# Signs written from the scaled words, and one softmax normalization per attention step for both query blocks

## The chip, the cores and the metric

The kernel runs on one core of a Trainium2 chip. The metric is the device time of one execution in microseconds; a change counts by the median of several executions. All times below are of that core. Engine names: PE is TensorE (PEld its weight loads), DVE is VectorE, ACT is ScalarE, POOL is GpSimd, SP is SyncE, which here only issues DMAs.

## What is computed

Causal attention over a window of keys plus a few sink keys, then two feed-forward layers on its output.

```python
scores = scale * q @ k.T                       # q, k, v: (2, 8, 768, 64)
keep = is_sink | ((rel >= 0) & (rel < window)) # n_sink 4, window 128
scores = where(keep, scores, -1e9)
a = exp(scores - max(scores))
x = (a / (sum(a) + 1e-9)) @ v                  # -> (1536, 512)
h = maximum(x @ w_in, 0);  x = h * h @ w_out   # 512 -> 2048 -> 512
h = x @ w_in2
out = (P(h) / (Q(h) + 1e-6)) @ w_out2          # P of degree 3, Q of degree 2 in |h|
```

The weights of the feed-forward layers arrive as float64, so every weight word is 8 bytes in HBM.

## The kernel before

**Attention** runs in 24 steps (2 batches, 3 pairs of 128-row query blocks, 4 pairs of heads). A step (`attention`, L304 to L391) is a generator with four pieces. The first two pieces are one query block each (`qb`): PE writes the scores of two heads to PSUM (L329 to L332), DVE adds the mask and takes the row maximum (L340, L341), ACT takes the exponential in place in `e` and sums the row (L348), DVE adds the guard and takes the reciprocal of two sums (L349, L350), and POOL multiplies the block's 320 columns by it (L352). The third piece transposes `e` on PE (`pt`, `sx`, L357 and L360) and lets POOL split it (L366, L367); the fourth multiplies with the values (`xo`, L382 to L386) and writes `xh` and `xl`, which the feed-forward part reads.

**Weights.** A chunk is one of 16 slices of `w_in` and `w_out` of a layer, 32 chunks in all (`load_chunk`, L292); it is loaded in two halves of 128x512 float64 words, 512 KB each. `narrowed` (L53) turns a half into float32: a DMA brings the raw words to `wr` (3 buffers), ACT multiplies the upper 32-bit words by 2^-112 into `t` (tile `wt`, 2 buffers, L63), ACT writes their signs, as the upper half of a zeroed word, into one of two sign tiles (L65), DVE shifts the lower words and adds the sign (L66, in place in `wr`), and DVE shifts `t` and adds that (L67). ACT then rounds to `wh` (L299) and POOL takes the rest, `wl` (L300). After that the half's `wt` buffer is free; its `wr` buffer is free after L67.

**Feed-forward.** 114 units, numbered here from 0: units 0 to 35 (256 tokens wide, 6 chunks, run among the attention steps), 36 to 65 (the rest of the first layer, 512 wide) and 66 to 113 (the second layer). A unit has 12 matmuls to `h` (L400), an activation on ACT, DVE and POOL (`squared_relu`: `sq`, L128 on ACT and L130 on DVE; then `gh` and `gl`, L407 and L409), and 12 matmuls to `acc` (L439 or L441). A unit's `h` is made two or three units ahead of its `acc`. There are 11 chunk slots, so chunks are loaded in bursts: 14 halves at the start, and then as the last use of a chunk frees its slot: around units 33 to 46, 50 to 55, 66 to 76 and 82 to 91.

**Order.** Each engine runs its instructions strictly in order. The order is set when the program is built: a list scheduler with a timeline model of the engines places the instructions of all generators, so a change in one instruction's inputs moves others on all engines. POOL, ACT and DVE serve attention, weights and units from one queue each.

Of the kernel before, what the change touches and what calls it, by code (L numbers as in the profile page):

```python
# [10 lines left out]
F16 = mybir.dt.float16  # L11
# [3 lines left out]
ALU = mybir.AluOpType  # L15
# [5 lines left out]
P = 128  # L21
# [7 lines left out]
GUARD = 1e-9  # L29
# [11 lines left out]
def f32(ap):  # L41
    return ap.bitcast(F32)
# [10 lines left out]
def narrowed(nc, pool, src, n, signs):  # L53

    raw = pool.tile([P, 512, 2], U32, tag="wr", name=f"wr{n}", bufs=3)
    nc.sync.dma_start(raw.rearrange("p c w -> p (c w)"), src.bitcast(U32))
    lo, hi = raw[:, :, 0], raw[:, :, 1]
    t = pool.tile([P, 512], U32, tag="wt", name=f"wt{n}")
    s = signs[0]
    signs.append(signs.pop(0))  # L60


    nc.scalar.mul(f32(t), f32(hi), 2.0**-112)  # L63

    nc.scalar.mul(s.bitcast(F16).rearrange("p (c w) -> p c w", w=2)[:, :, 1], f32(hi), 2.0**-112)  # L65
    nc.vector.scalar_tensor_tensor(out=lo, in0=lo, scalar=29, in1=s, op0=ALU.logical_shift_right, op1=ALU.bitwise_or)  # L66
    nc.vector.scalar_tensor_tensor(out=t, in0=t, scalar=3, in1=lo, op0=ALU.logical_shift_left, op1=ALU.bitwise_or)  # L67
    return f32(t)
# [107 lines left out]
def banded(ctx, tc, const, qk0, qk1, vb, vs, ns_f, win_f, wp, ab, scalars, out):  # L176
    nc = tc.nc
# [114 lines left out]
    def load_chunk(L, pool=wpool):  # L292
        home[L] = pool
        h = pool.tile([P, 1024], F32R, tag="wh", name=f"wh{L}")
        lo = pool.tile([P, 1024], F32R, tag="wl", name=f"wl{L}")
        for i in range(2):
            c = slice(i * 512, (i + 1) * 512)
            t = narrowed(nc, wraw, wp[L][:, c], f"{L}_{i}", signs)
            nc.scalar.copy(h[:, c], t)  # L299
            nc.gpsimd.tensor_tensor(out=lo[:, c], in0=t, in1=f32(h[:, c]), op=ALU.subtract)  # L300
        wh[L], wl[L] = h, lo


    def attention(bb, j, hp):  # L304

        n = f"{bb}_{j}_{hp}"
        nm = at.tile([P, 4], F32, tag="nm", name=f"nm{n}")
        sm = at.tile([P, 4], F32, tag="sm", name=f"sm{n}")
        rs = at.tile([P, 4], F32, tag="rs", name=f"rs{n}")
        W = P + SK  # L310

        e = at.tile([P, 2, 2 * W], F32, tag="e", name=f"e{n}")
        qk, kl, v = loaded[bb, j, hp]

        for qb in range(2):
            first = j == 0 and qb == 0
            nk = W if first else K0
            ss = []
            for hd in range(2):
                if hd == 0:  # L320
                    off = W * qb if j else 0
                else:
                    off = P if first else (W * (1 - qb) if j else 0)
                s = ps_at.tile([P, 512], F32, tag="at", name=f"s{n}_{qb}{hd}")
                cols = slice(qb * P, (qb + 1) * P)
                if kl is None:

                    rows = slice(hd * D, (hd + 1) * D)
                    nc.tensor.matmul(s[:, :nk], lhsT=qk[rows, cols], rhs=qk[rows, 256 + off : 256 + off + nk], start=True, stop=True)  # L329
                else:  # L330
                    nc.tensor.matmul(s[:, :nk], lhsT=qk[hd][:, cols], rhs=qk[hd][:, 256 + off : 256 + off + nk], start=True, stop=False)
                    nc.tensor.matmul(s[:, :nk], lhsT=qk[hd][:, cols], rhs=kl[hd][:, off : off + nk], start=False, stop=True)  # L332
                ss.append(s)
            for hd, s in enumerate(ss):
                u = 2 * qb + hd

                lo = 0 if hd == 0 or first else P
                if not first:
                    prev, own = (s[:, 0:P], s[:, W:K0]) if hd == 0 else (s[:, W:K0], s[:, 0:P])
                    nc.vector.copy_predicated(prev, own_u, own)  # L340
                nc.vector.tensor_tensor_reduce(  # L341
                    out=e[:, qb, hd * W : (hd + 1) * W], in0=s[:, lo : lo + W], in1=add[min(2 * j + qb, 2)][:, SK * (1 - hd) : SK * (1 - hd) + W],
                    scale=-SCALE, scalar=3.0e38, op0=ALU.add, op1=ALU.min, accum_out=nm[:, u : u + 1])
            c = slice(2 * qb, 2 * qb + 2)
            for hd in range(2):
                u = 2 * qb + hd
                eu = e[:, qb, hd * W : (hd + 1) * W]
                nc.scalar.activation(eu, eu, AF.Exp, bias=nm[:, u : u + 1], scale=-1.0, accum_out=sm[:, u : u + 1])  # L348
            nc.vector.tensor_scalar(out=rs[:, c], in0=sm[:, c], scalar1=GUARD, scalar2=None, op0=ALU.add)  # L349
            nc.vector.reciprocal(rs[:, c], rs[:, c])  # L350
            eq = e[:, qb, :].rearrange("p (h w) -> p h w", h=2)
            nc.gpsimd.tensor_tensor(out=eq, in0=eq, in1=rs[:, c].unsqueeze(2).to_broadcast([P, 2, W]), op=ALU.mult)  # L352
            yield
        pt = ps_at.tile([P, 4, P], F32, tag="at", name=f"pt{n}")
        for u in range(4):
            c0 = 0 if u < 2 else W + SK
            nc.tensor.matmul(pt[:, u, :], lhsT=e[:, u % 2, c0 : c0 + P], rhs=ident, is_transpose=True, start=True, stop=True)  # L357
        sx = ps_at.tile([P, 256], F32, tag="at", name=f"sx{n}")
        for qb in range(2):
            nc.tensor.matmul(sx[:, qb * P : (qb + 1) * P], lhsT=e[:, qb, P : 2 * P], rhs=ident, is_transpose=True, start=True, stop=True)  # L360

        pT = at.tile([P, 4, 2, P], F32, tag="pT", name=f"pT{n}", bufs=1)
        pa = at.tile([P, 4, P], F32, tag="pa", name=f"pa{n}", bufs=1)
        sT = at.tile([P, 256], F32R, tag="sT", name=f"sT{n}")
        nc.scalar.copy(pa, pt)
        nc.gpsimd.affine_select(out=pT[:, :, 1, :], in_=pa, pattern=[[0, 4], [1, P]], compare_op=ALU.is_ge, fill=0.0, base=0, channel_multiplier=-1)  # L366
        nc.gpsimd.affine_select(out=pT[:, :, 0, :], in_=pa, pattern=[[0, 4], [-1, P]], compare_op=ALU.is_gt, fill=0.0, base=0, channel_multiplier=1)  # L367

        half = slice(0, 2 * SK)
        nc.scalar.copy(sT[half], sx[half])  # L370
        nc.vector.tensor_tensor(out=sT[2 * SK :], in0=sx[half], in1=f32(sT[half]), op=ALU.subtract)
        yield
        xo = ps_at.tile([P, 256], F32, tag="at", name=f"xo{n}")
        pf = pT.rearrange("p (h q) o c -> p h (q o c)", q=2)
        nb = 2 if j == 0 else 3

        jobs = [(nb - 2, 0, 256, P), (nb - 1, P, 256, 3 * P)]
        if j:
            jobs.append((0, 0, P, 0))
        for i, c0, c1, o in jobs:  # L380
            for hd in range(2):
                nc.tensor.matmul(xo[64 * hd : 64 * hd + 64, c0:c1], lhsT=v[:, i, hd * D : (hd + 1) * D],  # L382
                                 rhs=pf[:, hd, o : o + c1 - c0], start=c1 - c0 == 256, stop=False, skip_group_check=True)
        vh, vl = vst[bb]
        nc.tensor.matmul(xo, lhsT=vh[:, hp, :], rhs=sT, start=False, stop=False, skip_group_check=True)  # L385
        nc.tensor.matmul(xo, lhsT=vl[:, hp, :], rhs=sT, start=False, stop=True, skip_group_check=True)  # L386
        t0 = bb * S + j * 256
        g, c0 = t0 // 512, t0 % 512
        nc.scalar.copy(xh[g][:, hp, c0 : c0 + 256], xo)
        nc.vector.tensor_tensor(out=xl[g][:, hp, c0 : c0 + 256], in0=xo, in1=f32(xh[g][:, hp, c0 : c0 + 256]), op=ALU.subtract)  # L390
        yield  # L391
# [99 lines left out]
    def att_pieces():  # L491
        live = {}
        for t in range(len(todo) + 2):
            for s_ in (t, t - 1, t - 2):
                if s_ < 0 or s_ >= len(todo):
                    continue
                if s_ == t:
                    live[s_] = attention(*todo[s_])
                    if fetch:
                        load_pair(*fetch.pop(0))  # L500
                    for _ in range(2):
                        next(live[s_])
                        yield
                else:
                    next(live[s_])
                    yield
            if t >= 2:
                done[t - 2] = True
# [226 lines left out]
```

## Time and profile before

| | us |
|---|---|
| median of 3 runs (lowest, highest) | 687.01 (686.88, 688.39) |
| the profiled execution | 685.88 |
| its span, first to last instruction | 684.2 |
| PE busy | 648.0 (95%) |
| DVE busy | 467.9 (68%) |
| ACT busy | 460.1 (67%) |
| POOL busy | 401.5 (59%) |

The profiled execution is 1.7 us longer than its span, and 1.1 us below the median of the runs. A busy PE does not mean a PE at its peak, since matmuls overlap in the pipeline; how many matmuls a stretch holds says more. In the rows, "x" is a count, ns after a comma a mean, and an arrow in brackets names what ended an idle time. SPq is the queue of DMA issues on SP.

### The profile page before, as it was taken

What the parts mean: (1) busy time and instruction counts of PE and PEld (TensorE: products, weight loads), DVE (VectorE), ACT (ScalarE), POOL (GpSimd) and SP (SyncE); (2) the same over time, 40 slices, a digit from 0 to 9 for tenths busy, and PEclk for the clock granted to TensorE, in tenths of its full rate; (3) what the DMA queues carried; (4) which work ended last, traced back from release to release, by engine and by line L of the source; (5) the groups of instructions that cost most, each with busy time, mean ns of one, the idle gap of its engine ahead of it and who ended that gap; (6) DMA issues with size and microseconds to landing.
All of it is one profiled execution on the core that took longest, in us unless ns stands there. A gap on an engine that the chain in (4) does not pass through costs nothing.

```text
span 684.2 us, 10131 instructions
## 1 busy us (share of the span) xinstructions
PE 648.0 (95%) x3376; PEld 528.2 (77%) x3376; DVE 467.9 (68%) x969; ACT 460.1 (67%) x938; POOL 401.5 (59%) x367
## 2 busy tenths in 40 slices
PE   4799999999999997999999998899998999999995
PEld 2456779999999875888778886688887888888884
DVE  7878855879842897427631279976699777577674
ACT  6767755777654876427542489886899866766761
POOL 4757855788753776327454579654577644544441
PEclk9999999999999999899999999999999999999998
DMA  7546632354200645204500033200030000001011
GB/s 249 186 134 184 204 90 69 103 135 131 67 25 1 210 160 182 65 1 137 171 0 1 0 124 103 82 1 1 1 123 32 0 1 1 0 1 61 3 61 68
DMA packets 25725, 54.16 MB, mean 79 GB/s; under 512 B 2880, under 2 KB 11072, under 8 KB 25664
## 3 DMA queue, kind: packets, MB, share of 16 engines
q1 hardware_dynamic: 25664, 53.43, 24.5%
q8 instruction: 29, 0.48, 0.3%
q14 instruction: 32, 0.26, 0.1%
HBM read 50.27 MB, written 3.15 MB: 78 GB/s over the span
## 4 chain that ended last, share of the span: by engine, by line
PE 63%; DVE 16%; ACT 8%; DMA 7%; issue 3%; POOL 2%; DVEq 0%; POOLq 0%; ACTq 0%
PE h L400 27%; PE acc L441 14%; PE acc L439 13%; DMA wr<-in_wp 6%; DVE wt L67 5%; DVE wr L66 4%; PE xo L382 3%; ACT sign L65 2%; PE pt L357 1%; PE s L329 1%; ACT wh L299 1%; ACT wt L63 1%; PE xo L385 1%; PE s L332 1%; POOL wl L300 1%
## 5 line engine op out<-in xcount | busy, mean ns | idle before, releaser
L409 POOL TENSOR_TENSOR gl<-sq,gh 128x256 fp32r<-128x256 f32 (+1 forms) x66 | 72.0, 1093 | 80.3 <-ACT gh L407 45.8
L164 POOL TENSOR_TENSOR z<-z,u 128x512 f32<-128x512 f32 x48 | 63.6, 1326 | 84.8 <-ACT z L163 81.5
L300 POOL TENSOR_TENSOR wl<-wt,wh 128x512 fp32r<-128x512 f32 x64 | 91.4, 1439 | 19.9 <-ACT wh L299 19.9
L66 DVE SCALAR_TENSOR_TENSOR wr<-wr,sign 128x512 uint32<-128x512 uint32 x64 | 64.2, 1003 | 19.6 <-ACT sign L65 19.5
L409 POOL TENSOR_TENSOR gl<-z,gh 128x512 fp32r<-128x512 f32 x47 | 62.1, 1322 | 24.8 <-ACT gh L407 21.2
L67 DVE SCALAR_TENSOR_TENSOR wt<-wt,wr 128x512 uint32<-128x512 uint32 x64 | 68.4, 1069 | 10.9 <-ACT wt L63 10.3
L130 DVE TENSOR_TENSOR sq<-sq,h 128x256 f32<-128x256 f32 (+1 forms) x66 | 35.5, 538 | 58.9 <-ACT sq L128 58.1
L439 PE MATMUL acc<-gh,wh 128*128 128x256 f32 (+1 forms) x264 | 66.2, 339 | 5.6 <-ACT sq L128 4.1
L65 ACT ACTIVATE sign<-wr 128x512 f16<-128x512 f32 x64 | 50.6, 790 | 24.6 <-DMA wr<-in_wp 24.4
L439 PE MATMUL acc<-gl,wh 128*128 128x256 f32 (+1 forms) x264 | 64.9, 336 | 0.5 <-POOL gl L409 0.5
L439 PE MATMUL acc<-gh,wl 128*128 128x256 f32 (+1 forms) x264 | 64.7, 334 | 0.0
L170 DVE SCALAR_TENSOR_TENSOR z<-z,con,h 128x512 f32<-128x512 f32 x48 | 35.8, 745 | 41.6 <-ACT h L169 40.1
L400 PE MATMUL h<-xh,wh 128*128 128x256 f32 (+1 forms) x264 | 61.6, 347 | 0.5 <-DVE sq L130 0.5
L128 ACT ACTIVATE sq<-h 128x256 f32<-128x256 f32 (+1 forms) x66 | 31.5, 477 | 45.3 <-PE h L400 34.5
L441 PE MATMUL acc<-wh,gh 128*128 128x512 f32 x192 | 60.2, 393 | 1.2 <-ACT gh L407 1.2
L441 PE MATMUL acc<-wl,gh 128*128 128x512 f32 x192 | 59.6, 390 | 0.0
L400 PE MATMUL h<-x2h,wh 128*128 128x512 f32 x192 | 53.9, 398 | 4.6 <-DVE z L172 4.6
L400 PE MATMUL h<-xl,wh 128*128 128x256 f32 (+1 forms) x264 | 58.2, 337 | 0.0
L400 PE MATMUL h<-xh,wl 128*128 128x256 f32 (+1 forms) x264 | 58.2, 338 | 0.0
L441 PE MATMUL acc<-wh,gl 128*128 128x512 f32 x192 | 57.6, 389 | 0.0
L439 PEld LDWEIGHTS acc<-gh,wh 128*128 128x128 f32 x264 | 44.5, 192 | 13.4 <-ACT wh L299 4.8
L352 POOL TENSOR_TENSOR e<-e,rs 128x320 f32<-128x320 f32 x48 | 37.2, 778 | 28.0 <-DVE rs L350 20.4
(104 smaller groups left out, 1591.9 us busy)
## 6 DMA issues: line engine op xcount, KB each, us to landing
wr<-in_wp SPq DMA_DIRECT2D x64, 512.0 KB, 3.7
qkr<-in_qk SPq DMA_DIRECT2D x32, 176.0 KB, 3.1
v<-in_vb SPq DMA_DIRECT2D x16, 192.0 KB, 2.7
out<-accsb SPq DMA_DIRECT2D x12, 256.0 KB, 2.1
qkr<-in_qk SPq DMA_DIRECT2D x8, 352.0 KB, 3.5
qkr<-in_qk SPq DMA_DIRECT2D x16, 136.0 KB, 2.8
qkr<-in_qk SPq DMA_DIRECT2D x4, 272.0 KB, 5.0
v<-in_vb SPq DMA_DIRECT2D x8, 128.0 KB, 3.6
```

The lines of the kernel that those rows point to most:

```text
L65: nc.scalar.mul(s.bitcast(F16).rearrange("p (c w) -> p c w", w=2)[:, :, 1], f32(hi), 2.0**-112)
L66: nc.vector.scalar_tensor_tensor(out=lo, in0=lo, scalar=29, in1=s, op0=ALU.logical_shift_right, op1=ALU.bitwise_or)
L67: nc.vector.scalar_tensor_tensor(out=t, in0=t, scalar=3, in1=lo, op0=ALU.logical_shift_left, op1=ALU.bitwise_or)
L130: nc.vector.tensor_tensor(out=r, in0=r, in1=h, op=ALU.mult)
L164: nc.gpsimd.tensor_tensor(out=z, in0=z, in1=u, op=ALU.mult)
L170: nc.vector.scalar_tensor_tensor(out=z, in0=z, scalar=con[:, 2:3], in1=h, op0=ALU.add, op1=ALU.mult)
L300: nc.gpsimd.tensor_tensor(out=lo[:, c], in0=t, in1=f32(h[:, c]), op=ALU.subtract)
L352: nc.gpsimd.tensor_tensor(out=eq, in0=eq, in1=rs[:, c].unsqueeze(2).to_broadcast([P, 2, W]), op=ALU.mult)
L400: nc.tensor.matmul(h[:, :n], lhsT=w_[:, k * P : (k + 1) * P], rhs=x_[:, k, c0 : c0 + n], start=p_ + k == 0, stop=p_ + k == 5)
L409: eng.tensor_tensor(out=gl[:, :n], in0=y, in1=f32(gh[:, :n]), op=ALU.subtract)
L439: nc.tensor.matmul(acc[m][:, :n], lhsT=w_[:, 512 + m * P : 512 + (m + 1) * P], rhs=g_[:, :n], start=st, stop=sp, skip_group_check=True)
L441: nc.tensor.matmul(acc[m], lhsT=g_[:, m * P : (m + 1) * P], rhs=w_[:, 512:1024], start=st, stop=sp)
```

## The change

Two edits. In `narrowed`, the sign activation reads `t`, the already scaled upper words, instead of the raw upper words. `t` is contiguous, the raw words stand 8 bytes apart; the value that is written is the same. In `attention`, the guard, the reciprocal and the multiplication by it are issued once per step, after the exponentials of both query blocks, over 4 sums and 640 columns instead of twice over 2 sums and 320 columns.

```diff
-    nc.scalar.mul(s.bitcast(F16).rearrange("p (c w) -> p c w", w=2)[:, :, 1], f32(hi), 2.0**-112)
+    nc.scalar.mul(s.bitcast(F16).rearrange("p (c w) -> p c w", w=2)[:, :, 1], f32(t), 1.0)
...
-            c = slice(2 * qb, 2 * qb + 2)
...
-            nc.vector.tensor_scalar(out=rs[:, c], in0=sm[:, c], scalar1=GUARD, scalar2=None, op0=ALU.add)
-            nc.vector.reciprocal(rs[:, c], rs[:, c])
-            eq = e[:, qb, :].rearrange("p (h w) -> p h w", h=2)
-            nc.gpsimd.tensor_tensor(out=eq, in0=eq, in1=rs[:, c].unsqueeze(2).to_broadcast([P, 2, W]), op=ALU.mult)
+            if qb:
+                nc.vector.tensor_scalar(out=rs, in0=sm, scalar1=GUARD, scalar2=None, op0=ALU.add)
+                nc.vector.reciprocal(rs, rs)
+                eq = e.rearrange("p q (h w) -> p (q h) w", h=2)
+                nc.gpsimd.tensor_tensor(out=eq, in0=eq, in1=rs.unsqueeze(2).to_broadcast([P, 4, W]), op=ALU.mult)
```

The exponential moves from L348 to L347; the other lines named here keep their numbers. The scheduler orders every engine anew. Two places follow.

DVE in the first attention step (names end in batch_pair_headpair and a buffer number; `s` are scores, `nm` maxima, `sm` and `rs` sums and reciprocals). Before:

```order
L340 COPY_PREDICATED s_0_0_11_180<-own_u,s_0_0_11_180 128x128
L349 TENSOR_SCALAR rs_0_0_165<-sm_0_0_164 128x2
L341 ISA e_0_0_166,nm_0_0_163<-s_0_0_11_180,add_116 128x160
L341 ISA nm_0_0_163 128x1
L341 ISA e_0_1_258,nm_0_1_255<-s_0_1_00_259,add_115 128x160
L341 ISA nm_0_1_255 128x1
L350 RECIPROCAL rs_0_0_165<-rs_0_0_165 128x2
```

Now:

```order
L340 COPY_PREDICATED s_0_0_11_177<-own_u,s_0_0_11_177 128x128
L341 ISA e_0_0_166,nm_0_0_163<-s_0_0_11_177,add_116 128x160
L341 ISA nm_0_0_163 128x1
L341 ISA e_0_1_255,nm_0_1_252<-s_0_1_00_256,add_115 128x160
L341 ISA nm_0_1_252 128x1
L341 ISA e_0_1_255,nm_0_1_252<-s_0_1_01_258,add_115 128x160
L341 ISA nm_0_1_252 128x1
L349 TENSOR_SCALAR rs_0_0_165<-sm_0_0_164 128x4
L350 RECIPROCAL rs_0_0_165<-rs_0_0_165 128x4
```

The first query block's guard and reciprocal are gone, and the step's only pair stands behind the maxima of the next step. Counted over the whole order of DVE, ahead of the L130 of unit 2 there were 16 L66, 15 L67 and 18 L350, and there are now 14, 13 and 8; ahead of that of unit 8 there were 19 L66, 16 L67 and 23 L350, and now 16, 16 and 11. Three signs (L65) that ACT wrote ahead of unit 8, before a buffer of `wt` was free for them, stand behind unit 32 now.

ACT in the second burst of weights, from the activation L128 of unit 41 to that of unit 42 (`wr15_1` is the second half of chunk 15). Before:

```order
L128 ACTIVATE sq_3499<-h_3484 128x512
L299 CAST wh14_3290<-wt14_0_3294 128x512
L299 CAST wh14_3290<-wt14_1_3303 128x512
L407 CAST gh_3465<-sq_3467 128x512
L65 ACTIVATE sign1_94<-wr15_1_3321 128x512
L63 ACTIVATE wt15_0_3314<-wr15_0_3312 128x512
L65 ACTIVATE sign0_93<-wr16_0_3332 128x512
L63 ACTIVATE wt15_1_3323<-wr15_1_3321 128x512
L299 CAST wh15_3310<-wt15_0_3314 128x512
L128 ACTIVATE sq_3531<-h_3516 128x512
```

Now:

```order
L128 ACTIVATE sq_3427<-h_3412 128x512
L299 CAST wh13_3198<-wt13_0_3202 128x512
L407 CAST gh_3393<-sq_3395 128x512
L63 ACTIVATE wt13_1_3211<-wr13_1_3209 128x512
L65 ACTIVATE sign1_94<-wt13_1_3211 128x512
L63 ACTIVATE wt14_0_3222<-wr14_0_3220 128x512
L65 ACTIVATE sign0_93<-wt14_0_3222 128x512
L128 ACTIVATE sq_3459<-h_3444 128x512
```

Before, ACT had written the sign of a half, and sometimes of the next, before its `t`; now the sign stands behind its `t`, and at the same unit the weights are one to two chunks further back. Counted over the whole order of ACT, 26 L63 stood ahead of unit 40, 36 ahead of unit 44 and 36 ahead of unit 46; now 25, 32 and 36. In the burst at units 50 to 55 it is 36 ahead of unit 50 and 46 ahead of unit 55, before and now. Ahead of units 66 and 74 it was 49 and 56 and is 48 and 56; the last 8 stand ahead of unit 88 before and ahead of unit 90 now.

## Rows read from the trace of the kernel before

**Rows 1.** The page: the span.
```profile
span 684.2 us, 10131 instructions
```

**Rows 2.** Stages: us, then busy us (count) of PE, PEld, DVE, ACT, POOL; PEclk, DMA, GB/s.
```profile
0.00:85.00 85.00, 68.14 (x318) 44.83 (x319) 70.30 (x233) 61.59 (x171) 56.17 (x64) 0.98 0.60 193
85.00:205.00 120.00, 120.00 (x995) 108.81 (x994) 85.75 (x307) 79.27 (x240) 84.77 (x110) 1.00 0.33 88
...
260.00:280.00 20.00, 15.40 (x57) 11.71 (x56) 14.02 (x19) 12.53 (x23) 10.82 (x9) 0.83 0.52 172
280.00:305.00 25.00, 25.00 (x110) 20.35 (x109) 7.22 (x11) 7.19 (x12) 6.43 (x5) 1.00 0.05 19
305.00:345.00 40.00, 38.46 (x168) 30.98 (x167) 26.05 (x31) 26.61 (x45) 23.94 (x17) 1.00 0.39 132
...
395.00:440.00 45.00, 40.98 (x176) 32.43 (x175) 41.35 (x53) 40.93 (x70) 35.81 (x25) 1.00 0.34 117
...
490.00:530.00 40.00, 38.23 (x166) 30.77 (x165) 35.89 (x46) 37.58 (x65) 29.68 (x22) 1.00 0.20 66
```

**Rows 3.** The chain that ended last, followed back from 85 us: shares, two pieces.
```profile
by line: DMA wr<-in_wp 10.9%; DVE wr L66 8.5%; DVE wt L67 6.1%; PE s L329 5.9%; ACT e L348 5.7%; ACT sign L65 5.7%; PE xo L382 5.3%; DVE rs L349 4.7%; issue 4.1%; PE h L400 3.9%; DMA raw<-in_nw 3.6%; DVE e L341 2.9%; DVE s L340 2.7%; PE pt 
...
54.99 4.41 DMA wr<-in_wp
...
69.40 4.88 DMA wr<-in_wp
```

**Rows 4.** Stages of L349 alone: us, DVE busy us (count), then as in rows 2.
```profile
0.00:40.00 40.00, 4.33 (x9) 1.00 0.60 200
40.00:80.00 40.00, 4.55 (x9) 0.99 0.60 188
```

**Rows 5.** The same of L350.
```profile
0.00:40.00 40.00, 1.42 (x9) 1.00 0.60 200
40.00:80.00 40.00, 1.47 (x9) 0.99 0.60 188
```

**Rows 6.** Timeline of DVE and of POOL: start us, us, engine, line, operation.
```profile
17.09 1.23 DVE L349 TENSOR_SCALAR rs<-sm 128x2 f32<-128x2 f32 x1
...
14.91 3.39 POOL L300 TENSOR_TENSOR wl<-wt,wh 128x512 fp32r<-128x512 f32 x2
```

**Rows 7.** Line L352: ns min/median/max, who waited (us, times); two in the timeline.
```profile
L352 POOL TENSOR_TENSOR e<-e,rs x48: 712/722/1192, 10.3 to 196.1; 128x320 f32<-128x320 f32 x48
...
  PEld pt L357: 2.3, 3
...
152.33 1.40 POOL L352 TENSOR_TENSOR e<-e,rs 128x320 f32<-128x320 f32 x2 [0.83 <-DVE rs L349]
```

**Rows 8.** Groups by line of the narrowing: busy us, mean ns; idle before.
```profile
L66 DVE SCALAR_TENSOR_TENSOR wr<-wr,sign 128x512 uint32<-128x512 uint32 x64 | 64.2, 1003 | 19.6 <-ACT sign L65 19.5
...
L65 ACT ACTIVATE sign<-wr 128x512 f16<-128x512 f32 x64 | 50.6, 790 | 24.6 <-DMA wr<-in_wp 24.4
...
L63 ACT ACTIVATE wt<-wr 128x512 f32<-128x512 f32 x64 | 42.3, 663 | 4.4 <-POOL wl L300 4.2
...
L299 ACT CAST wh<-wt 128x512 fp32r<-128x512 f32 x64 | 38.9, 617 | 11.5 <-DVE wt L67 11.4
```

**Rows 9.** The chain between bursts: one unit's matmuls (start us, us).
```profile
285.62 2.75 PE acc L439 x12
288.37 2.80 PE h L400 x12
```

**Rows 10.** Timeline of SP's queue, from 195 us: the second burst's DMA issues.
```profile
221.88 56.64 SPq L56 DMA_DIRECT2D wr<-in_wp  x20
```

**Rows 11.** Timeline of ACT and PE where PE stood longest in that burst.
```profile
270.29 0.78 ACT L65 ACTIVATE sign<-wr 128x512 f16<-128x512 f32 x1 [1.43 <-DMA wr<-in_wp]
...
271.95 0.59 ACT L128 ACTIVATE sq<-h 128x512 f32<-128x512 f32 x1
272.53 0.76 PE L439 MATMUL acc<-gh,wh 128*128 128x512 f32 x1 [4.05 <-ACT sq L128]
```

## The prediction

> **What bounds the kernel now.** I read the page first, then busy time by stage, then the chain inside the stages that are not full, then single lines. The span is 684.2 us [rows 1]; the stages [rows 2] show three kinds of stretch. To 85 us PE does 318 matmuls in 68 busy us while DVE is busy for 70.3 of 85 us: this is the start, in which attention and the first seven chunks share DVE and ACT. From 85 to 205 us PE is busy without a gap, and all other engines have at least 28% to spare. Behind that PE is full but for four stretches, which are the bursts of weights. A full stretch holds 110 matmuls in 25 us, 0.227 us each. By that price PE loses 20 - 57 x 0.227 = 7.1 us from 260 to 280, 1.9 from 305 to 345, 5.0 from 395 to 440 and 2.3 from 490 to 530 us: 16.3 us in all. In the first of these the granted clock is 0.83 over the stretch: the stall of 4.05 us [rows 11] is followed by matmuls at the lower of the two levels, 1.2 instead of 2.4 GHz, and part of the 7.1 us is that.
>
> So the end moves only if the start gets shorter, or the four bursts lose less or more. Between them nothing can be gained on DVE, ACT or POOL.
>
> **The start: one normalization instead of two.** L349 and L350 run 18 times each to 80 us and take 4.33 + 4.55 and 1.42 + 1.47 us [rows 4, 5], 11.8 us in all. Half of them go: 5.9 us of DVE, the upper bound of the gain. The lower bound is nothing, if something other than DVE ends the stage. The chain up to 85 us [rows 3] gives L349 4.7%, which is 4.0 us; half of that is 2.0, and with a part of the reciprocals I take **-3**.
>
> The multiplication on POOL takes 0.72 us for 320 columns, and two of them back to back 1.40 us [rows 7]. Over 640 columns I take 1.40 us. POOL saves next to nothing (24 x 0.04, about 1 us of an engine with room). But the transposes now wait for a multiplication that begins only behind both blocks and is 1.40 - 0.72 = 0.68 us longer. PE waited for L352 only 3 times, 2.3 us in all [rows 7]; all three can get longer by 0.68, which bounds this at 0 to +2.0; I take **+0.7**. From 85 to 205 us I cost it at nothing: PE has units to run there, and the transposes stand no earlier in PE's order than before. If that cover failed, 14 steps would cost 0.68 each, 9.5 us.
>
> **The start: the sign behind t.** A half's sign used to start when its DMA landed; now t comes first, 0.66 us [rows 8]. Reading contiguous words may make the sign cheaper, by 0.663 - 0.617 = 0.05 us if reading is what separates t from the cast L299, and by 0.17 at most, if it became as short as L299. I take 0.05, 3 us of ACT over 64 halves, which nothing waits for. The chain of the start goes through two DMAs of raw words that a sign then waits for [rows 3]; each gets 0.66 us longer: **+1.2** (0 to +3.5, if all five rounds of 16 halves through 3 buffers showed it). In the other direction, three signs and their L66 leave the start (19 ahead of unit 8, now 16): 3 x 0.79 us of ACT and 3 x 1.0 us of DVE [rows 8], between 0 and -3.0; **-1**. They return in the burst, where they count below. Sum of the start: -3 + 0.7 + 1.2 - 1 = **-2.1**, between -8.9 and +5.5.
>
> **The bursts.** A raw buffer goes round: DMA, ACT, L66, L67, and the next DMA is issued from SP's queue when L67 frees it. In the second burst 20 issues take 56.64 us [rows 10], 2.83 us per half. With three buffers, 0.66 us more per round is 0.22 us more per half: 3.05. A unit takes 2.75 + 2.80 = 5.55 us of PE [rows 9]. Before, ACT's order has 10 halves between the activations of units 40 and 44; they take 28.3 us where four units take 22.2, so PE falls 6.1 us behind, which is most of its 7.1. The rows show how: L128 of unit 43 stands behind a sign that waits for its DMA and behind two casts, and PE waits 4.05 us for it [rows 11]. Now 11 halves stand between units 40 and 46: 33.6 us against 33.3, so PE would hardly fall behind, and the drop of the clock would go with the stall. The bounds are -7.1 (all of it) and +4.4 (20 halves by 0.22, nothing else changed). I take **-4.5**, not the full 6, since port and DMA waits scatter by more than the 0.3 us of margin.
>
> In the burst at units 50 to 55 the order keeps two halves per unit, so its 10 halves get 10 x 0.22 = 2.2 us slower; the lead of `h` over `acc` has room for a part: **+1.5** (0 to +2.2). In the two bursts of the second layer DVE and ACT are each busy for over 40 of 45 us [rows 2] and the change takes nothing from DVE there; the last one is spread over two more units: **-0.5** together (-3 to +3).
>
> **The sum** is -2.1 - 4.5 + 1.5 - 0.5 = -5.6 us against the profiled execution's own 685.9 us, so 680.3. That execution lies 1.1 us under the median of the runs shown, 687.0; carried over, the median becomes **681.4 us**.
>
> **A rule that speaks against it.** DVE's L349 has only 2 columns, and yet it took 1.23 us at 17.09, and ended within 0.02 us of POOL's L300 pair [rows 6]: a small DVE instruction stands until POOL is through. One multiplication of 1.40 us can hold it twice as long in one piece as one of 0.72. The Trainium skill, page "SBUF — State Buffer", section "SBUF: two separate sides", says that DVE and GpSimd share a port pair as an exclusive lock for a whole instruction, the loser blocking fully; by this rule the trace agrees, since L349 waits and does not merely slow down. It is a rival below.
>
> **Rivals.** (1) *Everything comes through*: the start gains its 5.9 + 3.0 and the burst its 7.1, so 670 to 675 us. For it: DVE is the busiest engine of the start. Against: two DMA links and PE's own pieces stand in that chain. 14%. (2) *No difference*: the start is held by the weights, and what DVE gives up is taken by the longer way of each half, while the new order meets the same waits: 685.7 to 688.3 us. For it: the DMA and the four narrowing steps are the largest part of the chain of the start. 13%. (3) *Slower, by the wait of the sign for t in the bursts*: the 48 halves that come behind the start, by 0.22 us, are +10.6; less the 2.1 of the start, and with no other gain in the second burst, the time is 695; with half of the 10.6, 690. It decides where halves come slower than one per 2.8 us (half a unit) while the order asks for two per unit, that is in units 50 to 55 first. For it: all four bursts already lose time. Against: the order now asks for halves later. 17%. (4) *The longer hold of DVE by POOL*: ten steps of the start by 0.7 us, +7.0, and the sum becomes +1.4: 688.4 us. For it: the row of L349 above. Against: the number of DVE instructions that can be held falls as well. 6%. That the change does not do what it says can be left out, since the order shows 24 pairs for 48.
>
> **How the numbers follow.** The forecast, between 676 and 685.6 us, has 50%. About 0.2% (1.4 us) is what a measurement of this kernel can tell from no change. Faster is the forecast and (1), 0.64; the same is (2), 0.13; slower are (3) and (4), 0.23. For the range I leave out most of (1) and the worse half of (3): 675 to 690 us.
>
> **What would show it.** In the profile after: 24 L349 and L350 on DVE, with some 6 us less to 80 us; L352 at 1.3 to 1.5 us; the sign at 0.7 to 0.8 us, behind its t; PE gapless from about 83 us; no stall of over 2 us near unit 43 and a granted clock of 1.00 there; a rate of 3.0 to 3.1 us per issue in the second burst. Wrong would be: PE gapless no earlier than now, a stall of several us in units 50 to 55, or halves that come at well over 3.1 us.

## The result and the profile after

The changed kernel takes **665.6 us** (665.3 to 666.5, 4 runs) where the kernel before, timed beside it, took 686.9 us (684.9 to 688.4): a ratio of **0.969**, 95% interval 0.967 to 0.972. It is faster by 21 us. The forecast was 681.4 us, between 675 and 690: the sign was right, the size was not. The profiled execution took 665.9 us.

The page of the changed kernel: its span, busy time by engine, and the chain that ended last, by engine.

```profile
span 663.8 us, 10100 instructions
...
PE 638.2 (96%) x3376; PEld 522.7 (79%) x3376; DVE 455.6 (69%) x921; ACT 460.2 (69%) x938; POOL 394.6 (59%) x343
...
PE 76%; ACT 9%; DVE 8%; issue 3%; POOL 2%; DMA 1%; SPq 0%; DVEq 0%; POOLq 0%; ACTq 0%
```

The stages of the changed kernel, as in [rows 2].

```profile
0.00:85.00 85.00, 68.37 (x356) 45.10 (x356) 64.48 (x213) 61.58 (x171) 54.27 (x55) 0.92 0.58 187
85.00:205.00 120.00, 120.00 (x1017) 110.97 (x1017) 82.20 (x278) 77.85 (x240) 82.46 (x96) 1.00 0.33 92
...
260.00:280.00 20.00, 19.73 (x85) 15.58 (x84) 14.94 (x20) 14.54 (x25) 12.58 (x9) 1.00 0.41 142
305.00:345.00 40.00, 40.00 (x174) 32.49 (x173) 22.41 (x32) 22.55 (x38) 22.36 (x16) 1.00 0.32 106
395.00:440.00 45.00, 43.96 (x188) 34.80 (x187) 44.62 (x61) 43.01 (x73) 36.33 (x26) 1.00 0.23 82
490.00:530.00 40.00, 40.00 (x174) 32.51 (x174) 36.69 (x53) 36.46 (x62) 25.93 (x20) 1.00 0.08 27
```

By the price of the forecast (0.227 us per matmul) the four stretches of the bursts now lose 0.7, 0.5, 2.3 and 0.5 us, 4.0 in all, where they lost 16.3; the windows are the same, though the bursts now begin 7 to 17 us earlier. The start has 356 matmuls to 85 us instead of 318, but at a clock of 0.92 instead of 0.98.

Where the 21 us came from is read from the units' activations (L128, L159) in ACT's timeline, of one profiled execution of each kernel. Those of units 0, 24, 48, 66 and 113, the last, before:

```profile
58.05 0.36 ACT L128 ACTIVATE sq<-h 128x256 f32<-128x256 f32 x1
...
186.75 0.39 ACT L128 ACTIVATE sq<-h 128x256 f32<-128x256 f32 x1 [0.24 <-PE h L400]
...
296.81 0.60 ACT L128 ACTIVATE sq<-h 128x512 f32<-128x512 f32 x1 [3.14 <-PE h L400]
...
399.29 0.58 ACT L159 ACTIVATE u<-h 128x512 f32<-128x512 f32 x1
...
665.94 0.58 ACT L159 ACTIVATE u<-h 128x512 f32<-128x512 f32 x1
```

The same five now:

```profile
54.75 0.39 ACT L128 ACTIVATE sq<-h 128x256 f32<-128x256 f32 x1
...
180.12 0.38 ACT L128 ACTIVATE sq<-h 128x256 f32<-128x256 f32 x1
...
282.87 0.60 ACT L128 ACTIVATE sq<-h 128x512 f32<-128x512 f32 x1 [2.71 <-PE h L400]
...
383.23 0.59 ACT L159 ACTIVATE u<-h 128x512 f32<-128x512 f32 x1
...
645.26 0.58 ACT L159 ACTIVATE u<-h 128x512 f32<-128x512 f32 x1
```

At unit 24 the start is over and PE is full. The start gave 6.6 us, the stretch behind it with its four bursts 14.0 us: 7.3 to unit 48 (the second burst of weights), 2.1 to unit 66 (the burst at units 50 to 55) and 4.6 to unit 113 (the two bursts of the second layer). Each run below has the same split. The kernel before took between 682.9 and 691.7 us in its runs, so what is read from one execution of it is uncertain by some us. The parts behind the start repeat better: among the runs with the changed sign in the bursts they agree within 1.5 us, but for o1_behind between units 24 and 48.

The steps of the normalization in the changed kernel: first L349 to 40 and to 80 us, as in [rows 4].

```profile
0.00:40.00 40.00, 1.09 (x4) 0.93 0.63 207
40.00:80.00 40.00, 1.36 (x5) 0.90 0.56 175
```

The same of L350, as in [rows 5].

```profile
0.00:40.00 40.00, 0.69 (x4) 0.93 0.63 207
40.00:80.00 40.00, 0.87 (x5) 0.90 0.56 175
```

L352, as in [rows 7], and the last row of who waited for it.

```profile
L352 POOL TENSOR_TENSOR e<-e,rs x24: 1246/1253/1689, 11.5 to 188.5; 128x640 f32<-128x640 f32 x24
...
  PE pt L357: 4.6, 3
```

Before, PE itself never waited for L352; the row of [rows 7] is of weight loads (PEld), 2.3 us, which are 6.5 us now. DVE saved 11.8 - 4.0 = 7.8 us to 80 us, more than the 5.9 that I had as the upper bound, and yet the start gained less than that. The narrowing's lines in the changed kernel, as in [rows 8]:

```profile
L66 DVE SCALAR_TENSOR_TENSOR wr<-wr,sign 128x512 uint32<-128x512 uint32 x64 | 66.5, 1039 | 35.7 <-ACT sign L65 35.4
...
L65 ACT ACTIVATE sign<-wt 128x512 f16<-128x512 f32 x64 | 50.5, 789 | 0.8
L63 ACT ACTIVATE wt<-wr 128x512 f32<-128x512 f32 x64 | 42.7, 667 | 10.6 <-POOL wl L300 8.1 <-DMA wr<-in_wp 2.3
L299 ACT CAST wh<-wt 128x512 fp32r<-128x512 f32 x64 | 39.2, 618 | 22.8 <-DVE wt L67 21.8 <-PE acc L439 0.8
```

The sign itself is no cheaper (789 ns for 790). What is gone is ACT's 24.4 us of waiting for a DMA at the sign; `t`, now in front, waits 2.3 us for a DMA and otherwise, 8.1 us, for a `wt` buffer. A part of the idle time has only moved: at the cast L299 ACT now waits 21.8 us for DVE, where it was 11.4 [rows 8].

### The profile page after: what moved, and what is told of

Read it like the earlier page. It is cut to its first block, busy times and chain, and to the rows that moved or that the text cites. A ratio compares the mean times of both kernels' runs of the same rounds, so it can differ in the third digit from the quotient of the medians.

```text
span 663.8 us, 10100 instructions
## 1 busy us (share of the span) xinstructions
PE 638.2 (96%) x3376; PEld 522.7 (79%) x3376; DVE 455.6 (69%) x921; ACT 460.2 (69%) x938; POOL 394.6 (59%) x343
## 4 chain that ended last, share of the span: by engine, by line
PE 76%; ACT 9%; DVE 8%; issue 3%; POOL 2%; DMA 1%; SPq 0%; DVEq 0%; POOLq 0%; ACTq 0%
PE h L400 34%; PE acc L439 17%; PE acc L441 15%; PE xo L382 3%; DVE wr L66 3%; DVE wt L67 2%; ACT sign L65 1%; ACT wt L63 1%; PE pt L357 1%; PE s L329 1%; PE s L332 1%; PE xo L385 1%; PE s L331 1%; ACT z L163 1%; ACT wh L299 1%
## 5 line engine op out<-in xcount | busy, mean ns | idle before, releaser
L300 POOL TENSOR_TENSOR wl<-wt,wh 128x512 fp32r<-128x512 f32 x64 | 89.0, 1397 | 40.9 <-ACT wh L299 38.9
L66 DVE SCALAR_TENSOR_TENSOR wr<-wr,sign 128x512 uint32<-128x512 uint32 x64 | 66.5, 1039 | 35.7 <-ACT sign L65 35.4
L130 DVE TENSOR_TENSOR sq<-sq,h 128x256 f32<-128x256 f32 (+1 forms) x66 | 35.4, 538 | 49.1 <-ACT sq L128 48.5
L67 DVE SCALAR_TENSOR_TENSOR wt<-wt,wr 128x512 uint32<-128x512 uint32 x64 | 64.4, 1006 | 3.4
L128 ACT ACTIVATE sq<-h 128x256 f32<-128x256 f32 (+1 forms) x66 | 31.3, 474 | 42.5 <-PE h L400 32.1
L400 PE MATMUL h<-xh,wl 128*128 128x256 f32 (+1 forms) x264 | 56.8, 334 | 0.0
L299 ACT CAST wh<-wt 128x512 fp32r<-128x512 f32 x64 | 39.2, 618 | 22.8 <-DVE wt L67 21.8
L400 PE MATMUL h<-x2l,wh 128*128 128x512 f32 x192 | 53.5, 396 | 0.0
L400 PE MATMUL h<-x2h,wl 128*128 128x512 f32 x192 | 53.2, 396 | 0.0
```

What stands on the lines that cost most here:

```text
L128: nc.scalar.activation(r, h, AF.Relu)
L130: nc.vector.tensor_tensor(out=r, in0=r, in1=h, op=ALU.mult)
L400: nc.tensor.matmul(h[:, :n], lhsT=w_[:, k * P : (k + 1) * P], rhs=x_[:, k, c0 : c0 + n], start=p_ + k == 0, stop=p_ + k == 5)
```

## Experiments

Three theories stood at first. **A**: a sign that stands ahead of its `t` in ACT's order waits for its DMA there, and activations that PE needs stand behind it. **B**: the sign behind `t` makes each half longer (the forecast's view), and the gain is the softmax's. **C**: the gain is the contiguous source, or a lucky order. All runs, each timed beside the kernel before, with the split as above ("start" to the activation of unit 24, "rest" from there to unit 113, then the three parts of the rest; us against the trace of the kernel before):

| run | median us | ratio, 95% interval | start | rest | 24 to 48 | 48 to 66 | 66 to 113 |
|---|---|---|---|---|---|---|---|
| changed kernel | 665.63 | 0.969 (0.967 to 0.972) | -6.6 | -14.0 | -7.3 | -2.1 | -4.6 |
| e1_sign | **658.71** | 0.960 (0.954 to 0.965) | -15.4 | -11.9 | -6.2 | -2.1 | -3.6 |
| e2_softmax | 687.65 | 1.000 (0.997 to 1.003) | +3.3 | -1.9 | -2.5 | -0.3 | +0.8 |
| e3_order | 667.08 | 0.972 (0.967 to 0.978) | -10.0 | -9.5 | -7.1 | -2.6 | +0.2 |
| e3_hold | 673.70 | 0.981 (0.976 to 0.986) | -3.4 | -8.8 | -0.7 | -3.1 | -4.9 |
| g1_early | 667.88 | 0.972 (0.968 to 0.977) | -6.3 | -12.9 | -6.2 | -2.1 | -4.6 |
| g2_late | 658.88 | 0.959 (0.955 to 0.963) | -14.1 | -14.1 | -7.3 | -2.1 | -4.6 |
| f1_pool | 669.03 | 0.973 (0.969 to 0.977) | -3.4 | -13.3 | -7.6 | -2.1 | -3.6 |
| f2_dve | 666.70 | 0.969 (0.965 to 0.973) | -6.6 | -13.3 | -7.6 | -2.1 | -3.6 |
| k1_first | 674.87 | 0.983 (0.978 to 0.988) | -14.7 | +2.1 | -0.7 | 0.0 | +2.7 |
| k2_rest | 673.66 | 0.980 (0.976 to 0.983) | +0.2 | -12.9 | -6.3 | -2.1 | -4.6 |
| m_warm | 668.48 | 0.972 (0.969 to 0.976) | -4.6 | -13.0 | -7.3 | -2.1 | -3.5 |
| o1_behind | 663.30 | 0.966 (0.963 to 0.969) | -11.2 | -10.5 | -4.8 | -2.1 | -3.6 |
| o2_behind_b | 684.87 | 0.997 (0.994 to 1.000) | -1.5 | +0.5 | -1.0 | 0.0 | +1.6 |

### The two edits apart

**e1_sign** has the first hunk of the change alone (L65), **e2_softmax** the second alone (L349 to L352).

> The sign edit alone; two normalizations per step stay. Theory A (the gain of about 14 us behind the start comes from ACT no longer standing at a sign that waits for its DMA, ahead of activations that PE needs): 671 to 676 us, waits of signs for DMA on ACT under 5 us in all where the kernel before has 24.4, PE idle in the four bursts under 4 us together. Theory B (a half takes one step longer, so that the bursts get slower, and the gain is the softmax's): 688 to 695 us.

> One normalization per step alone; the sign reads the raw words as before. Theory A: only the start gains, 679 to 683 us, and the signs still wait about 24 us for DMAs. Theory B: most of the gain is here, 666 to 670 us.

The sign edit alone gives 658.7 us, 7 us *less* than both edits together; the merged normalization alone gives nothing. B falls. A's ranges were missed too: e1_sign lies 12 us under its 671 to 676, and e2_softmax has none of the gain that 679 to 683 us meant.

### What it is about the sign

**e3_order** leaves the sign reading the raw words and only queues it behind its `t` on ACT; **e3_hold** lets it go ahead of `t`, but only when the half that used its sign tile last, two halves before, has been split into `wh` and `wl`.

The edit of e3_order, at L63 and L65:

```diff
-    nc.scalar.mul(f32(t), f32(hi), 2.0**-112)
+    scaled = nc.scalar.mul(f32(t), f32(hi), 2.0**-112)
+    with TC[0].issue_after(scaled.ins):
-    nc.scalar.mul(s.bitcast(F16).rearrange("p (c w) -> p c w", w=2)[:, :, 1], f32(hi), 2.0**-112)
+        nc.scalar.mul(s.bitcast(F16).rearrange("p (c w) -> p c w", w=2)[:, :, 1], f32(hi), 2.0**-112)
```

That of e3_hold, in `load_chunk` behind L300, where POOL puts the zero that the sign tile's first word has anyway:

```diff
+            z = f32(lo[:, i * 512 : i * 512 + 1])
+            nc.gpsimd.tensor_tensor(out=f32(signs[-1])[:, 0:1], in0=z, in1=z, op=ALU.subtract)
```

> The kernel before, with one edge of order added: the sign still reads the raw words, but is issued behind its own t on ACT. Two normalizations stay. Theory A: what counts is that the sign stands behind t, which needs a free buffer, so this does what the sign edit alone does, within 3 us of that run, 671 to 677 us. Theory C (the contiguous source or the new data dependency itself, or merely another order that came out well, makes the gain): 683 to 690 us.

> The kernel before, with 64 small POOL instructions added: behind the last step of a half, POOL writes the first word of that half's sign tile to zero, so that the next sign in this tile waits until that half is through, as t does for its buffer, but not for t. Two normalizations stay. Theory A: the holding back is what counts, 671 to 680 us (64 small instructions on POOL included). Theory C: 685 to 695 us.

Both gain without the contiguous source, by two different orders, so C falls as the whole of the cause. It does not fall as a part of it. e3_order was expected within 3 us of e1_sign and lies 8.4 us above it: between units 24 and 66 it gains no less (9.7 us), but its start is 5.4 us short, and in the second layer it gains nothing (+0.2, e1_sign -3.6). e3_hold has most of its gain behind unit 48. What ACT's signs and `t` waited for in whole executions (us, times, longest), in the kernel before:

```profile
ACT sign L65 <- DMA wr<-in_wp: 24.4, 23, 2.6
...
ACT wt L63 <- POOL wl L300: 4.2, 8, 0.7
```

The same in e3_order, where no sign or `t` waited for a DMA (L66 is L63 there):

```profile
ACT wt L66 <- POOL wl L304: 10.0, 16, 1.3
```

A sign tile comes free early (L66 of two halves ago), so the order put signs up to three ahead of their `t`, and 23 of the 64 waited there for their DMA. A `t` needs a `wt` buffer, which POOL frees late; by then the raw words have mostly landed, and what is left is a wait for POOL. With the sign behind `t`, no half gets ahead of that.

### By place

**k1_first** uses the sign edit in the first 16 halves, **k2_rest** in the other 48.

```diff
+    HALF[0] += 1
+    src_, f_ = (t, 1.0) if HALF[0] <= 16 else (hi, 2.0**-112)
-    nc.scalar.mul(s.bitcast(F16).rearrange("p (c w) -> p c w", w=2)[:, :, 1], f32(hi), 2.0**-112)
+    nc.scalar.mul(s.bitcast(F16).rearrange("p (c w) -> p c w", w=2)[:, :, 1], f32(src_), f_)
```

In k2_rest the condition is `HALF[0] > 16`.

> The sign reads the scaled words (behind its t) in the first 16 halves alone, those of the start; the other 48 halves and the normalization as before. If the gain of the sign edit adds up over places, as the times of the units in the traces say (about 15 us by the seventh unit, about 12 us more in the bursts): 671 to 676 us. If the gain of the start is eaten up later by the bursts, because units that come earlier find their weights later: 680 to 688 us.

> The sign reads the scaled words in halves 17 to 64 alone, those of the bursts; the start and the normalization as before. If the gain adds up over places: 674 to 679 us, and ACT's waits of a sign for its DMA are left in the start alone. If a sign behind its t makes each half of a burst slower, as the forecast had it: 686 to 695 us.

The gain adds up to within about 3 us: 12.6 us (687.5 - 674.9) and 13.8 us (687.5 - 673.7), and 29.6 for both places in e1_sign. What PE waited for from 205 to 530 us, the stretch of the four bursts, in the kernel before:

```profile
PE h L400 <- DVE z L172: 4.6, 3, 2.3
PE acc L439 <- ACT sq L128: 4.1, 1, 4.1
PE acc L439 <- ACT gh L407: 1.5, 1, 1.5
PE acc L441 <- ACT gh L407: 1.2, 1, 1.2
PE acc L439 <- POOL gl L409: 0.5, 1, 0.5
```

The same in k2_rest, where these lines stand 5 or 6 further down:

```profile
PE acc L445 <- ACT wh L305: 1.2, 1, 1.2
PE h L406 <- DVE z L177: 1.1, 3, 0.6
```

PE's waits went from 11.9 us to 2.3; in k1_first they stand as before (12.8 us). In the two bursts of the first layer A holds: 18.8 of the 20.6 us that signs waited for DMAs from 205 to 530 us lie there, at 16 signs, among L128 and L407, and e3_order, which keeps the raw words, has the whole gain there. The Trainium skill, page "PSUM — Partial Sum Buffer", section "Engine vs sequencer instructions", says that the queues of ScalarE, VectorE and GpSimdE are strict FIFO; the trace agrees, as L128 at 271.95 us stood behind a sign that had waited 1.43 us for its DMA [rows 11]. In the changed kernel the same unit's L128 stands behind a `t` that waited 0.39 us, and PE does not wait; ACT's timeline there:

```profile
257.01 0.80 ACT L65 ACTIVATE sign<-wt 128x512 f16<-128x512 f32 x1
258.20 0.68 ACT L63 ACTIVATE wt<-wr 128x512 f32<-128x512 f32 x1 [0.39 <-POOL wl L300]
258.79 0.57 ACT L128 ACTIVATE sq<-h 128x512 f32<-128x512 f32 x1
```

In the second layer A is not shown. Signs waited there only three times, 1.7 us in all, in the kernel before (ACT's waits from 380 to 530 us):

```profile
ACT sign L65 <- DMA wr<-in_wp: 1.7, 3, 0.6
```

PE waits there mostly for L172 on DVE. The chain that ended last, before, from 405 us to the end of the longest of these waits at 436 us, runs mostly through DVE's own work and has no landing on it:

```profile
by line: DVE wt L67 20.3%; DVE wr L66 19.9%; DVE t L165 9.7%; DVE h L171 8.9%; DVE t L166 8.8%; issue 7.7%; DVE z L170 6.8%; DVE accsb L465 6.3%; DVE z L172 5.1%; ACT t L161 2.2%; ACT u L168 1.8%; ACT wh L299 1.7%; ACT u L159 1.6%; DVEq L66
```

And in e3_order, where no sign waits for a DMA, PE still waits for it from 380 to 530 us (L176 is L172 there):

```profile
PE h L404 <- DVE z L176: 3.6, 3, 2.0
```

So the 4.6 us of k2_rest behind unit 66 come with another order, perhaps that of L66 and L67 among DVE's steps of the units; no run parts this.

In the start the chain that ended last points the way of A. With the signs ahead, in k2_rest, it goes through these landings of raw words in mid-start, as it did before [rows 3]; in k1_first no landing of `wr` is on it.

```profile
55.44 4.51 DMA wr<-in_wp
...
69.73 4.57 DMA wr<-in_wp
```

But before, the signs of the start waited for DMAs only four times, 3.8 us in all, and the gain there is 14.7 us; where the rest comes from is not shown.

### Why the merged normalization costs

On top of the sign edit it costs 8.8 us in the start by the split, 6.9 in all by the medians. **Theory L**: the transposes (L357) wait for one multiplication behind both blocks; PE stands and its clock falls. **H**: POOL's longer piece holds DVE, rival 4 of the forecast. **O**: an accident of the order, anywhere. **g1_early** merges in attention steps 1 to 10 only, **g2_late** in steps 11 to 24. **f1_pool** merges the multiplication only, **f2_dve** L349 and L350 only, with two multiplications behind them. All four have the sign edit.

In g1_early a step counter decides between the code before and the code of the change (in g2_late by `> 10`):

```diff
+        STEP[0] += 1
+        one = STEP[0] <= 10
...
+            if not one:
...
+            elif qb:
```

In f1_pool L349 and L350 stay as before, and only the multiplication is that of the change:

```diff
             nc.vector.reciprocal(rs[:, c], rs[:, c])
-            eq = e[:, qb, :].rearrange("p (h w) -> p h w", h=2)
-            nc.gpsimd.tensor_tensor(out=eq, in0=eq, in1=rs[:, c].unsqueeze(2).to_broadcast([P, 2, W]), op=ALU.mult)
+            if qb:
+                eq = e.rearrange("p q (h w) -> p (q h) w", h=2)
+                nc.gpsimd.tensor_tensor(out=eq, in0=eq, in1=rs.unsqueeze(2).to_broadcast([P, 4, W]), op=ALU.mult)
```

In f2_dve the multiplication of the changed kernel is cut in two:

```diff
                 nc.vector.reciprocal(rs, rs)
-                eq = e.rearrange("p q (h w) -> p (q h) w", h=2)
-                nc.gpsimd.tensor_tensor(out=eq, in0=eq, in1=rs.unsqueeze(2).to_broadcast([P, 4, W]), op=ALU.mult)
+                for q in range(2):
+                    eq = e[:, q, :].rearrange("p (h w) -> p h w", h=2)
+                    nc.gpsimd.tensor_tensor(out=eq, in0=eq, in1=rs[:, 2 * q : 2 * q + 2].unsqueeze(2).to_broadcast([P, 2, W]), op=ALU.mult)
```

> The sign edit with the merged normalization in the first 10 attention steps alone (those of the first 85 us). Theory L (the 7 us that the merged normalization costs beside the sign edit arise in the start: transposes wait for one multiplication behind both blocks, PE goes idle and its clock falls): 663 to 668 us, as the changed kernel. Theory O (they come from another order of the instructions anywhere, the later steps included): 658 to 663 us.

> The sign edit with the merged normalization in steps 11 to 24 alone, while PE has units to run. Theory L: 656 to 661 us, no worse than the sign edit alone (658.7). Theory O: 661 to 668 us.

> The sign edit with L349 and the reciprocals for each block as before, and only POOL's multiplication in one piece of 640 columns behind both blocks. Theory L: 662 to 668 us, since the transposes wait as long as in the changed kernel. Theory H (the 1.27 us piece on POOL holds DVE at the shared port, and that is the price): 662 to 668 us too. If instead the merged L349 and reciprocals are the price: 656 to 661 us.

> The sign edit with one L349 and one reciprocal behind both blocks, and POOL's multiplication in two pieces of 320 columns behind them. Theory L: 662 to 668 us, since both multiplications begin only behind the second block. Theory H (the long piece on POOL): 656 to 661 us, since no piece of POOL is longer than in the sign edit alone.

The price lies wholly in the first 10 steps (667.9 against 658.9 us), and it is there however the work is cut, once the first block's part waits for the second (f1_pool, at 669.0 us, lies 1 us above its range). H falls: f2_dve has no piece on POOL longer than before and takes 666.7 us. Its two pieces can stand back to back, but DVE's L349 says the same: to 85 us it takes at most 0.59 us in the changed kernel, with 0.17 as the median, and 1.12 and 0.28 in e1_sign. PE's waits to 85 us in the changed kernel, the three largest; the wait for L352 in the second row is 2.9 us in f2_dve and 4.7 in f1_pool, and none in e1_sign or g2_late.

```profile
PE s L329 <- DMA qkr<-in_qk: 5.1, 1, 5.1
PE pt L357 <- POOL e L352: 4.6, 3, 2.4
PE s L329 <- DVE nm L341: 3.3, 4, 1.3
```

The stretch from 30 to 50 us, in the columns of [rows 2], of the changed kernel:

```profile
30.00:50.00 20.00, 15.12 (x60) 8.27 (x59) 13.37 (x42) 13.52 (x37) 11.91 (x11) 0.66 0.49 152
```

The same of e1_sign:

```profile
30.00:50.00 20.00, 18.26 (x115) 11.99 (x113) 19.00 (x64) 16.29 (x49) 14.95 (x17) 1.00 0.62 194
```

PE gets through 60 matmuls instead of 115: it stands 3.1 us longer, and much of what it does runs at 1.2 GHz. But the clock's fall did not come behind a wait for L352, as L had it. It came at 34.6 us, behind a wait for a maximum (L341); of the two long waits for L352 one lies 22 us ahead of that and the other 10 us behind it:

```profile
12.83 1.12 PE L357 MATMUL pt<-ident,e 128*128 128x128 f32 x4 [2.45 <-POOL e L352]
...
33.40 0.72 PE L329 MATMUL s<-qkr 64*128 64x288 f32 x2 [0.60 <-DVE nm L341]
...
44.98 1.12 PE L357 MATMUL pt<-ident,e 128*128 128x128 f32 x4 [1.80 <-POOL e L352]
```

And f2_dve, with 2.9 us of such waits, takes as long as the changed kernel with 4.6. That the merge in the first 10 steps is the price is shown; that the transposes' wait is what makes it is argued.

### Clock and order

**m_warm** puts four transposes of the identity ahead of the transposes of steps 2 to 8 of the changed kernel. **o1_behind** is the changed kernel with its first 14 halves queued behind the attention steps that e1_sign has ahead of them; **o2_behind_b** does that to the kernel before. **Theory Q** against L: the price, and the sign edit's gain in the start, are the order of halves against attention steps.

The edit of m_warm, ahead of L356 (`warm` is 4 in steps 2 to 8, else 0):

```diff
+        for _ in range(warm):
+            nc.tensor.matmul(pt[:, 0, :], lhsT=ident, rhs=ident, is_transpose=True, start=True, stop=True)
```

That of o1_behind at L63 (o2_behind_b has L65 in the block too); `EXPS` holds the last exponential of each step, and `k` is the entry of the half; the loop that loads chunks first runs attention on to that step:

```diff
+BEHIND = [None, 0, 1, 1, 2, 3, 4, 4, 5, 5, 6, 7, 7, 8]
...
-    nc.scalar.mul(f32(t), f32(hi), 2.0**-112)
+    with TC[0].issue_after(EXPS[k]) if k is not None else nullcontext():
+        nc.scalar.mul(f32(t), f32(hi), 2.0**-112)
```

> The changed kernel with four transposes of the identity ahead of the transposes of attention steps 2 to 8, so that PE has work while it waits for the one multiplication; their results are overwritten. If the lower clock from 35 to 50 us is the price of the merged normalization: 660 to 664 us. If it is the wait for the multiplication and the clock only follows it: 665 to 669 us, at a granted clock nearer to 1.00 in the start.

> The changed kernel, both edits, with one thing more: in the first 14 halves, each t is queued on ACT behind the exponentials of an attention step that the order of the sign edit alone has ahead of it, so that 10 halves and not 11 stand ahead of the first unit, and fewer ahead of each attention step. Theory Q (what the merged normalization costs in the start is the order that it makes: halves that stand ahead of attention steps): 656 to 662 us, as the sign edit alone. Theory L (the transposes' wait for one multiplication is the price itself, whatever the order): 664 to 669 us.

> The kernel before, with signs from the raw words ahead of their t and two normalizations, and its first 14 halves queued behind the same attention steps; the bursts as before. Theory Q (the sign edit's gain in the start is the order of halves against attention steps, not the in-order wait of a sign for its DMA): 673 to 678 us, as with the sign edit in the first 16 halves (674.9). If the wait of the signs for their DMA is what costs in the start: 682 to 689 us.

m_warm tells nothing of the clock's share: the clock fell all the same (0.83 from 20 to 40 us, 0.74 from 40 to 60), and the time did not fall. o1_behind takes 663.3 us, just under L's range and above Q's: its start is 4.6 us shorter than the changed kernel's, of the 8.8 that separate that from e1_sign. So about half of the price in the start goes with the order that the merge brings, with more halves ahead of each attention step; by the medians it gives back 2.3 of 6.9 us, since behind the start it gains 3.5 us less. That the other half is the wait is not shown; PE waits 2.9 us for the multiplication there. o2_behind_b lies in the range of the DMA wait, and Q falls for the sign edit's gain in the start; but its clock was at 0.74 from 20 to 40 us, where the kernel before had 1.00, so this run does not part the two cleanly.

## Why the prediction was wrong

**The bursts: the step that failed.** I gave them -4.5 + 1.5 - 0.5 = -3.5 us; they gave 14.0, and k2_rest, which changes them alone, 13.8. By the split the three terms came to -7.3, -2.1 and -4.6 us (-6.3, -2.1 and -4.6 in k2_rest). What failed is how I priced a sign that stands behind its `t`: as a longer way for every half, with one gain beside it. First, I read the stall of [rows 11] as a matter of one place, unit 43, and priced only that crossing. But the 24.4 us of ACT waiting for a DMA at the sign [rows 8], a row that I had, were spread over 23 signs, 18.8 us of them over 16 signs in both bursts of the first layer. Second, I charged 0.22 us per half for the longer way round the raw buffers, +1.5 in units 50 to 55 and the whole of rival 3. Halves did come slower, more than I had it: the 20 L67 of the second burst stand 2.95 us apart before (220.84 to 276.97 us) and 3.43 us now, by the first and last of them in the changed kernel:

```profile
214.14 0.69 DVE L67 SCALAR_TENSOR_TENSOR wt<-wt,wr 128x512 uint32<-128x512 uint32 x1
...
279.37 1.19 DVE L67 SCALAR_TENSOR_TENSOR wt<-wt,wr 128x512 uint32<-128x512 uint32 x1
```

I had called anything well over 3.1 a mark of failure. It cost nothing: the order asks for halves later, the next units' weights came in time, and PE had been held by the activations, not by the halves. Third, the -0.5 for the second layer came to -4.6. I had DVE and ACT busy for over 40 of 45 us in both of its bursts, which [rows 2] has only for the first (36 and 38 of 40 us in the other), and gave DVE's order no part; PE's waits there were for DVE. What the edit changed in that order stays open.

**The start: the right sign, wrong in both parts.** I had -2.1, and it gave 6.6. The merged normalization I took at -3 + 0.7; it costs 8.8 beside the sign edit, by the split. Alone it cost 3.3 there in one trace, and nothing in the medians. DVE's saving was real, 7.8 us, but DVE's share of the chain was not the price. The +0.7 for the transposes was bounded by three waits of 2.3 us that I took for PE's, and the row is of PEld. With both blocks to wait for, PE itself stood 4.6 us at three waits, and the order made more of it. "The lower bound is nothing" had excluded a loss without a reason. The sign edit I took at +1.2 - 1; it gives 14.7 in the start (k1_first). I had counted the landings on the chain as something that gets 0.66 us longer each, where putting the sign back takes them off the chain.

**What was right.** From 85 to 205 us the merge costs nothing (g2_late). Rival 4 is not the price (f2_dve). The drop of the clock near unit 43 went with its stall. The sign took 0.79 us, in the range given; L352 took 1.25 us in the median, just under its own. Rival 1 had the nearest time, and the 7.1 us of the second burst came as it says, but it counts on DVE's 5.9 us too, which gave nothing.

**Left open.** What makes the 4.6 us of the second layer. How the start's gain from the sign edit divides between the two landings, the order and the clock; e3_order, behind `t` but with raw words, has 10.0 us of the 14.7. Whether the clock's fall in the start adds to the price or only goes with it: g2_late also fell, to 0.83 from 30 to 50 us, and was not slower than e1_sign.

## What to carry to other kernels

In an engine's order, an instruction that can be ready only when a DMA lands should stand behind one that is held back by a buffer of its own, or everything behind it pays for the landing (shown here for the bursts of the first layer): sum an engine's waits for DMA over all bursts, and ask what stood behind each. Merging two small steps saves their cost, but the first block's consumers then wait for the second; here that cost nothing where PE had other work (steps 11 to 24) and was a loss where it had none. Time the edits of a change apart: here one alone is better than both.

## What was not expected of the hardware

Reading contiguous float32 words instead of every second one changed nothing for the sign (789 ns for 790), though `t`, from every second word, takes 667 ns and the cast from contiguous ones 618; so the sign's 0.12 us over `t` does not come from its source, which leaves its half-word output (not tried apart). On POOL one piece of 640 columns takes 1.25 us where two of 320 take 2 x 0.72, or 1.40 back to back [rows 7], so a piece carries some 0.15 to 0.19 us of its own. And in the start of the changed kernel PE's clock fell to 0.50 (1.2 GHz) at 35 us, behind a wait of PE of 0.60 us, and was back at 1.00 only at 49; 28 transposes of the identity in m_warm did not hold it up.
